# The first value block of a decode-attention kernel loaded by every eighth row instead of by column halves

## The chip, the cores and the metric

The kernel runs on one NeuronCore of a Trainium2 chip. The metric is device time in microseconds (us), from start to end of one execution; the median of several runs is given. The core has engines that run side by side: TensorE (PE, matrix products; PEld is its weight load), VectorE (DVE), ScalarE (ACT), GpSimd (POOL) and SyncE (SP), which here only issues loads. Loads and stores are carried out by 16 DMA engines that all issuing queues share.

## The reference

One query row per head attends to 8192 keys; there are 16 heads of 256 elements, all bfloat16.

```
B, H, Sq, Sk, D = 1, 16, 1, 8192, 256
scale = q.shape[-1] ** -0.5
scores = jnp.einsum("bhqd,bhkd->bhqk", q, k) * scale
p = _softmax(scores, axis=-1)
return jnp.einsum("bhqk,bhkd->bhqd", p, v)
```

Keys and values are 4 MB each per head, 134 MB together, and each byte is used once.

## The kernel before

**Layout.** The 8192 keys of a head are dealt to 128 partitions, 64 consecutive keys to each: partition p holds keys 64p to 64p + 63, which is one run of 64 x 256 elements or 32 KB in memory. J = 64 is the number of keys of a partition, D = 256 the elements of one. A "column" j of a block is the j-th key of every partition. There are two buffers for K and two for V (`kbuf`, `vbuf`); even heads use the first, odd heads the second.

**Work per head.** VectorE multiplies 48 of the 64 columns of K with the query and sums them (L191). TensorE does the other 16: it transposes them (L280), ScalarE copies the transposes out of the accumulators (L376), and TensorE multiplies them with the query (L294). VectorE takes the maximum (L207), TensorE transposes and broadcasts it (L228, L234) with a step of VectorE between (`xmax`, L173), ScalarE forms the exponentials and their sum. Then `pv` on TensorE (L259) adds up 64 products, one for each column of V, and ScalarE scales the row and stores it (`final`, L401). In one turn of TensorE's loop the order is: scores of an even head, `pv` of the even head two before, scores of the odd head, `pv` of the odd head two before. Within `pv` of an even head the maximum of the following odd head is transposed after 32 columns and broadcast after 48. VectorE's part of that broadcast, `xmax` of the odd head, comes after its column 40 of the next even head.

**The loads.** SP issues all loads of K and V from one list, `stream` (L57 to L71), in the order of the list, and the DMA engines carry them out in that order. An entry names the tensor, the head, the columns and the semaphore that counts its landing; each transfer adds 16. Heads 0 and 1 go into empty buffers. From head 2 on, the load of K waits until VectorE has finished with the buffer (`kd`), and the load of V until `pv` has (`pv`). The list begins: K0 in three pieces (columns 0 to 15, 16 to 31, 32 to 63), K1, the first half of V0's columns, K2, the second half of V0, the first half of V1, K3, the second half of V1; then K(h + 2) and V(h) in turn for h = 2, 3 and so on. V14 and V15, the last two, come in four and nine pieces of columns.

**The waits of `pv`.** The same code runs for all heads. It waits for `va0` or `va1` (the whole block, or its first piece), and then, before certain columns, for further semaphores of pieces (`v0c` before column 32 and so on; `V_SEMS`, `V_LATE`). Blocks that come whole need no such wait; GpSimd adds 16 to the piece semaphores once at the start (the list `late`), so that the waits pass for all heads but the last two. `v0c` and `v1c` are not in `late`, since V0's and V1's second halves add the 16 themselves.

Of the kernel before, what the change touches and what calls it, by code (L numbers as in the profile page):

```python
# [13 lines left out]
K_FIRST = (16, 32)  # L14
# [3 lines left out]
V_SEMS = (("va0", "v0b", "v0c", "v0d"), ("va1", "v1b", "v1c", "v1d", "v1e", "v1f", "v1g", "v1i", "v1j"))  # L18
# [22 lines left out]
def bass_standalone__mha_softmax__decode_kernel(nc: bass.Bass, q: bass.AP, k: bass.AP, v: bass.AP, out: bass.AP):  # L41
    B, H, Sq, D = q.shape
    Sk = k.shape[2]
    P = 128
    J = Sk // P
# [4 lines left out]
    JD = J - NPE  # L50
    QW = D + NH
    HALF = J // 2
    dt = k.dtype

    stream = [("k", 0, 0, K_FIRST[0], "k0"), ("k", 0, K_FIRST[0], K_FIRST[1], "k0a")]  # L57
    stream += [("k", 0, K_FIRST[1], J, "k0b"), ("k", 1, 0, J, "k1")]
    stream += [("v", 0, 0, HALF, "va0"), ("k", 2, 0, J, "k0"), ("v", 0, HALF, J, "v0c")]
    stream += [("v", 1, 0, HALF, "va1"), ("k", 3, 0, J, "k1"), ("v", 1, HALF, J, "v1c")]  # L60
    for h in range(2, H):
        if h + 2 < H:
# [4 lines left out]
        elif h == V_HALVED:  # L67
            stream += [("v", h, 0, HALF, "va1"), ("v", h, HALF, J, "v1h")]
        else:
            stream.append(("v", h, 0, J, f"va{h % 2}"))  # L70

    with contextlib.ExitStack() as ctx:

        def sb(name, shape, d):
            return ctx.enter_context(nc.sbuf_tensor(name, shape, d))
# [6 lines left out]
        def sem(name):  # L82
            if name not in sems:
                sems[name] = ctx.enter_context(nc.semaphore(name))
            return sems[name]

        kbuf = [sb(f"kbuf{i}", [P, J * D], dt) for i in range(2)]
        vbuf = [sb(f"vbuf{i}", [P, J * D], dt) for i in range(2)]
# [25 lines left out]
            sem(name)  # L114
        for name in ("l", "rc", "pv", "fin", "ldq", "k0", "k0a", "k0b", "k1", "va0", "va1", "v1h", "o0", "o1"):
            sem(name)
        late = [name for row in V_SEMS for name in row[1:] if name not in ("v0c", "v1c")] + ["v1h"]
        for row in V_SEMS:
            for name in row[1:]:
                sem(name)  # L120
# [1 line left out]
        def src(t, h):  # L122
            return t[0, h].rearrange("(p j) d -> p (j d)", p=P)

        if True:

            @(lambda f: f(nc.sync))
            def _(sp):
                for kind, h, a, b, name in stream:
                    buf = (kbuf if kind == "k" else vbuf)[h % 2]  # L130
                    if h >= 2 and a == 0:
                        if kind == "k":
                            sp.wait_ge(sem("kd"), h)
                        else:
                            sp.wait_ge(sem("pv"), h + 1)
                    sp.dma_start(  # L136
                        buf[:, a * D : b * D], src(k if kind == "k" else v, h)[:, a * D : b * D]
                    ).then_inc(sem(name), 16)
                sp.nop()
# [85 lines left out]
            def _(pe):  # L225
# [26 lines left out]
                def pv(h, waits, at):  # L252

                    pe.wait_ge(sem("fin"), h.of(1, 3))
                    pe.wait_ge(sem(f"va{h.par}"), h.of(8, 32 - 8 * h.par))
                    for j in range(J):
                        for name, value in waits.get(j, ()):
                            pe.wait_ge(sem(name), value)
                        ins = pe.matmul(  # L259
                            acc[h.par][0:1, 0:D],  # L260
                            lhsT=E[h.par][:, j : j + 1],
                            rhs=vbuf[h.par][:, j * D : (j + 1) * D],
                            start=(j == 0),
                            stop=(j == J - 1),
                        )
                        if j == J - 1:
                            ins.then_inc(sem("pv"), 1)
                        if j + 1 in at:
                            at[j + 1]()
# [76 lines left out]
                with pe.Fori(0, H // 2 + 1) as i:  # L346
                    ev, od = _Step(0, i), _Step(1, i)
                    fin_turn = pe.snap((i // 8) * 16 + 16)
                    half_turn = pe.snap(((i + 1) // 8) * 16 + 16)
                    old = od.back(2)  # L350
                    with pe.If(i < H // 2):
                        scores(ev)
                    with pe.If(i > 0):
                        pv(
                            ev.back(2),
                            {V_LATE[14][n]: [(V_SEMS[0][n], fin_turn)] for n in range(1, len(V_SEMS[0]))},
                            {32: lambda: transpose_m(old), 48: lambda: bcast(old), 64: lambda: total(old)},
                        )
                    with pe.If(i < H // 2):
                        scores(od, before=ev)  # L360
                    with pe.If(i > 0):
                        waits = {V_LATE[15][n]: [(V_SEMS[1][n], fin_turn)] for n in range(1, len(V_SEMS[1]))}
                        waits[HALF] = [("v1h", half_turn)]
                        pv(old, waits, {})
                    with pe.If(i < H // 2):
                        total(ev)
# [122 lines left out]
```

## Time and profile before

| | us |
|---|---|
| median of 3 runs | 320.06 (320.04 to 320.07) |
| the profiled execution | 320.12 |
| its span | 318.6 |
| VectorE busy | 275.2 (86%) |
| TensorE busy, weight loads | 219.2 (69%), 156.0 (49%) |
| ScalarE busy | 92.5 (29%) |
| bytes moved by the loads and stores | 134.29 MB, mean 422 GB/s |

The span runs from the first to the last instruction on the core; the execution's own time adds what lies around it. Busy times of different engines overlap. A row of a timeline gives the start, the time taken, the engine, the line of the kernel, the operation with the tile written and the tiles read, and the count; what stands in brackets is the idle time before it and what ended that. "SPq" is SP issuing loads: its time is that of issuing, not of the transfer. A row of the issues gives tensor, queue, count, KB of one and the median time from issue to landing in us. A row of the stretches gives its limits, its length, the busy time of each engine with the number of instructions, the granted TensorE clock, the busy share of the DMA engines and the rate in GB/s; a share may pass 1 a little, since an engine has more than one packet under way.

### The profile page before, as it was taken

How to read it: one execution, taken by the hardware profiler on the slowest of the kernel's cores; microseconds unless marked ns; L12 is line 12 of the kernel's file. 1: busy time of each engine (PE TensorE's matmuls, PEld its weight loads, DVE VectorE, ACT ScalarE, POOL GpSimd, SP SyncE). 2: the span in 40 equal slices, each digit the busy share in tenths (PEclk: the TensorE clock that was granted, in tenths of full speed). 3: DMA queues.
4: the chain of work that ended last, by engine and by line, in shares of the span. 5: the costliest groups of instructions: out<-in, count | busy, mean ns of one | idle time of the engine just before them, and what ended most of it. 6: DMA issues, size and time to landing. Idle time of an engine off the chain costs nothing.

```text
span 318.6 us, 6833 instructions
## 1 busy us (share of the span) xinstructions
PE 219.2 (69%) x2163; PEld 156.0 (49%) x2163; DVE 275.2 (86%) x1584; ACT 92.5 (29%) x172; POOL 1.6 (0%) x11
## 2 busy tenths in 40 slices
PE   4446185988775947949387482975739668497987
PEld 1335163656553634727256262663626446266664
DVE  3989999999999898897988979799798897979920
ACT  5436050333215050330505114051330603306010
POOL 1000000000000000000000000000000000000000
PEclk9999999659797875957879597695977859699999
DMA  7999999999999999999999999999999999999995
GB/s 303 447 418 465 393 455 407 448 416 448 412 448 428 428 444 411 453 412 453 420 436 440 416 448 407 453 416 449 424 432 444 411 449 416 444 405 428 419 416 201
DMA packets 6981, 134.29 MB, mean 422 GB/s; under 512 B 800, under 2 KB 1216, under 8 KB 1856
## 3 DMA queue, kind: packets, MB, share of 16 engines
q1 hardware_dynamic: 6912, 134.22, 98.6%
q8 instruction: 2, 0.03, 0.0%
q10 hardware_dynamic: 64, 0.02, 0.0%
q14 instruction: 3, 0.02, 0.0%
HBM read 134.23 MB, written 0.01 MB: 421 GB/s over the span
## 4 chain that ended last, share of the span: by engine, by line
DMA 64%; PE 19%; DVE 15%; SPq 1%; issue 1%; ACT 0%; DVEq 0%; ACTq 0%
DMA vbuf<-in_v_dram 58%; PE acc L259 18%; DVE kbuf L191 14%; DMA kbuf<-in_k_dram 7%; SPq L136 1%; DVE S L191 0%; DVE g L173 0%; PE sm L234 0%; ACT o_sb L401 0%; DVE recip L178 0%; DVEq L209 0%; DVEq L183 0%; PE qps L244 0%; DVE m L207 0%; ACTq L400 0%
## 5 line engine op out<-in xcount | busy, mean ns | idle before, releaser
L191 DVE CUSTOM_DVE_ANT_0 kbuf<-kbuf,q_now 128x256 bf16<-128x256 bf16 x768 | 268.4, 409 | 21.3 <-DMA kbuf<-in_k_dram 20.4
L259 PE MATMUL acc<-vbuf,E 128*1 128x256 bf16 x1024 | 147.1, 313 | 41.6 <-DMA vbuf<-in_v_dram 41.4
L259 PEld LDWEIGHTS acc<-vbuf,E 128*1 128x1 bf16 x1024 | 95.5, 95 | 86.2 <-DMA vbuf<-in_v_dram 44.4
L376 ACT ACTIVATE KT<-tp 128x1024 bf16<-128x1024 bf16 x64 | 62.3, 1021 | 46.4 <-PE tp L280 45.9
L191 DVE DVE_READ_ACCUMULATOR2_ANT S<- 128x1 f32 x768 | 55.2, 72 | 0.0
L280 PE MATMUL tp<-identb,kbuf 128*128 128x128 bf16 x512 | 42.2, 239 | 14.7 <-DMA kbuf<-in_k_dram 14.5
L280 PEld LDWEIGHTS tp<-identb,kbuf 128*128 128x128 bf16 x512 | 33.6, 107 | 18.1 <-DMA kbuf<-in_k_dram 12.1
L294 PE MATMUL spe<-q_now,KT 128*128 128x1 bf16 x512 | 22.9, 166 | 27.3 <-ACT KT L376 27.0
L294 PEld LDWEIGHTS spe<-q_now,KT 128*128 128x128 bf16 x512 | 18.1, 99 | 35.7 <-ACT KT L376 26.1
L401 ACT ACTIVATE o_sb<-acc,recip 1x256 bf16<-1x256 f32 x16 | 7.3, 458 | 87.0 <-PE acc L259 85.7
L384 ACT ACTIVATE negb<-sm 128x1 f32<-128x1 f32 x16 | 2.8, 174 | 83.8 <-PE sm L234 83.8
L173 DVE TENSOR_REDUCE g<-mx 1x1 f32<-1x128 f32 x16 | 4.4, 276 | 7.5 <-PE mx L228 7.5
L234 PE MATMUL sm<-g,ones_row 1*128 1x1 f32 x32 | 6.5, 268 | 5.0 <-DVE g L173 5.0
L228 PE MATMUL mx<-ident,m 128*1 128x128 f32 x32 | 6.5, 287 | 4.3 <-DVE m L207 4.3
L234 PEld LDWEIGHTS sm<-g,ones_row 1*128 1x128 f32 x32 | 5.1, 198 | 7.1 <-DVE g L173 5.6
L371 ACT ACTIVATE q_now<-q_all 128x258 bf16 x16 | 6.7, 418 | 0.1
L178 DVE RECIPROCAL recip<-qps 1x1 f32<-1x1 f32 x16 | 2.4, 152 | 3.9 <-PE qps L244 3.9
L388 ACT ACTIVATE E<-S,negb 128x64 bf16<-128x64 f32 x16 | 5.6, 348 | 0.5
L336 PE MATMUL acc<-q_sb,identb 16*128 16x256 bf16 x16 | 4.3, 404 | 0.8 <-ACT q_all L426 0.8
L228 PEld LDWEIGHTS mx<-ident,m 128*1 128x1 f32 x32 | 2.1, 82 | 5.1 <-DVE m L207 4.8
L426 ACT ACTIVATE q_all<-acc 128x512 bf16<-128x512 f32 x8 | 4.3, 592 | 0.6 <-PE acc L336 0.6
L380 ACT ACTIVATE S<-spe 128x16 f32<-128x16 f32 x16 | 2.9, 184 | 3.6 <-PE spe L294 3.6
(24 smaller groups left out, 18.5 us busy)
## 6 DMA issues: line engine op xcount, KB each, us to landing
kbuf<-in_k_dram SPq DMA_DIRECT2D x15, 4096.0 KB, 20.3
vbuf<-in_v_dram SPq DMA_DIRECT2D x11, 4096.0 KB, 28.7
vbuf<-in_v_dram SPq DMA_DIRECT2D x6, 2048.0 KB, 24.4
vbuf<-in_v_dram SPq DMA_DIRECT2D x5, 1024.0 KB, 14.8
kbuf<-in_k_dram SPq DMA_DIRECT2D x2, 1024.0 KB, 5.8
kbuf<-in_k_dram SPq DMA_DIRECT2D x1, 2048.0 KB, 11.3
vbuf<-in_v_dram SPq DMA_DIRECT2D x1, 768.0 KB, 10.2
vbuf<-in_v_dram SPq DMA_DIRECT2D x1, 640.0 KB, 11.3
```

The costliest lines, as they stand in the source:

```text
L173: dve.tensor_reduce(g[0:1, h.par : h.par + 1], mx[0:1, 0:P], AX.X, ALU.max).then_inc(sem("g"), 1)
L191: ins = dve.tensor_tensor_reduce(out=buf[:, j * D : (j + 1) * D], in0=buf[:, j * D : (j + 1) * D], in1=q_now[h.par][:, 0:D], scale=SCALE, ...
L228: pe.matmul(mx[0:1, 0:P], lhsT=m[:, h.par : h.par + 1], rhs=ident[:, :], start=True, stop=True).then_inc(sem("mT"), 1)
L234: pe.matmul(sm[:, 0:1], lhsT=ones_row[0:1, 0:P], rhs=g[0:1, h.par : h.par + 1], start=True, stop=True,).then_inc(sem("bc"), 1)
L259: ins = pe.matmul(acc[h.par][0:1, 0:D], lhsT=E[h.par][:, j : j + 1], rhs=vbuf[h.par][:, j * D : (j + 1) * D], start=(j == 0), stop=(j == J ...
L280: ins = pe.transpose(tp[gi % 2][:, b * D + hf * P : b * D + (hf + 1) * P], buf[:, j * D + hf * P : j * D + (hf + 1) * P], identb[:, :],)
L294: ins = pe.matmul(spe[:, c : c + 1], lhsT=KT[gi % 2][:, b * D + hf * P : b * D + (hf + 1) * P], rhs=q_now[h.par][:, D + hf : D + hf + 1], ...
L336: ins = pe.matmul(acc[pair % 2][:, (h % 2) * D : (h % 2 + 1) * D], lhsT=identb[0:H, h : h + 1].to_broadcast([H, P]), rhs=q_sb[:, :], start ...
L371: act.activation(out=q_now[h.par][:, :], in_=src_q, func=ACT.Copy).then_inc(sem("qb"), 1)
L376: act.activation(out=KT[gi % 2][:, :], in_=tp[gi % 2][:, :], func=ACT.Copy).then_inc(sem("kt"), 1)
L388: act.activation(out=E[h.par][:, :], in_=S[h.par][:, :], func=ACT.Exp, bias=negb[:, h.par : h.par + 1], scale=1.0, accum_out=lsum[:, h.par ...
L401: act.activation(out=o_sb[h.par][0:1, :], in_=acc[h.par][0:1, 0:D], func=ACT.Copy, scale=recip[0:1, h.par : h.par + 1],).then_inc(sem("fin ...
```

## The change

V0, the value block of head 0, is no longer loaded as two halves of columns into all 128 partitions (128 x 16 KB each). It is loaded by eight transfers. Transfer r takes the partitions r, r + 8, r + 16 and so on to r + 120, 16 of them, with their whole 32 KB. Transfer 0 stands at the very head of the list, ahead of K0; transfers 1 to 3 stand behind K1, where the first half was; transfers 4 to 7 behind K2, where the second half was. All eight count on `va0`, so that `pv` of head 0 waits for 144 (16 from GpSimd and eight times 16) before its first column, and the values of later even heads rise by the same amount. `v0c` joins the semaphores that GpSimd raises ahead. All else is as before; lines further down move by 6.

```
@@ -50,13 +50,15 @@
     HALF = J // 2
+    ROWS = P // 16
...
-    stream = [("k", 0, 0, K_FIRST[0], "k0"), ("k", 0, K_FIRST[0], K_FIRST[1], "k0a")]
+    stream = [("row", 0, 0, 1, "va0")]
+    stream += [("k", 0, 0, K_FIRST[0], "k0"), ("k", 0, K_FIRST[0], K_FIRST[1], "k0a")]
     stream += [("k", 0, K_FIRST[1], J, "k0b"), ("k", 1, 0, J, "k1")]
-    stream += [("v", 0, 0, HALF, "va0"), ("k", 2, 0, J, "k0"), ("v", 0, HALF, J, "v0c")]
+    stream += [("row", 0, 1, ROWS // 2, "va0"), ("k", 2, 0, J, "k0"), ("row", 0, ROWS // 2, ROWS, "va0")]
...
-        late = [name for row in V_SEMS for name in row[1:] if name not in ("v0c", "v1c")] + ["v1h"]
+        late = [name for row in V_SEMS for name in row[1:] if name != "v1c"] + ["v1h"]
...
                 for kind, h, a, b, name in stream:
+                    if kind == "row":
+                        for r in range(a, b):
+                            sp.dma_start(vbuf[0][r:P:ROWS, :], src(v, h)[r:P:ROWS, :]).then_inc(sem(name), 16)
+                        continue
...
-                    pe.wait_ge(sem(f"va{h.par}"), h.of(8, 32 - 8 * h.par))
+                    pe.wait_ge(sem(f"va{h.par}"), h.of(8, 144 - 120 * h.par))
```

## The prediction

> **What bounds the kernel now.** I read the page first: the busy times, the forty slices with their DMA rows, the queues and the shares of the chain.
>
> ```profile
> span 318.6 us, 6833 instructions
> PE 219.2 (69%) x2163; PEld 156.0 (49%) x2163; DVE 275.2 (86%) x1584; ACT 92.5 (29%) x172; POOL 1.6 (0%) x11
> ...
> DMA  7999999999999999999999999999999999999995
> ...
> q1 hardware_dynamic: 6912, 134.22, 98.6%
> ...
> DMA 64%; PE 19%; DVE 15%; SPq 1%; issue 1%; ACT 0%; DVEq 0%; ACTq 0%
> ```
>
> The 16 DMA engines are full in every slice but the first and the last: SP's queue moves 134.22 MB and its packets fill 98.6% of the span. VectorE has 14% to spare, TensorE more. To price bytes I took stretches of the busy times: the start, the long middle, the end (the last column is GB/s).
>
> ```profile
> 0.00:2.50 2.50, 0.00 (x0) 0.00 (x0) 0.00 (x0) 1.28 (x1) 1.56 (x11) 1.00 0.35 53
> 2.50:5.00 2.50, 1.29 (x7) 0.62 (x7) 0.00 (x0) 0.83 (x4) 0.00 (x0) 1.00 0.96 396
> ...
> 82.50:302.50 220.00, 155.78 (x1568) 111.84 (x1569) 198.71 (x1145) 59.91 (x114) 0.00 (x0) 0.80 1.00 431
> 302.50:314.50 12.00, 10.92 (x95) 7.32 (x92) 2.00 (x12) 1.08 (x4) 0.00 (x0) 1.00 1.00 404
> ```
>
> 134.22 MB at the 431 GB/s of the middle take 311.4 us. The load stream begins near 2 us and ends near 314.5, so under 2 us of it are idle. The chain's last pieces show what follows the loads:
>
> ```profile
> 312.33 1.25 PE acc L259 x10
> ...
> 313.62 3.28 PE acc L259 x26
> ...
> 316.97 0.47 ACT o_sb L401
> ```
>
> Head 15's value products run behind its last chunks. This tail hangs on the last loads, so whatever makes the load stream longer makes the span longer by the same time.
>
> **The change, part by part.** The reader needs where SP issues what, and when it lands: first SP's queue in order of time, then issues with their time to landing (K1, V0's first half, K2, K3, V1's second half, K4; each line from a short stretch around its issue).
>
> ```profile
> 0.74 2.03 SPq L136 DMA_DIRECT2D kbuf<-in_k_dram  x4
> 2.81 0.44 SPq L136 DMA_DIRECT2D vbuf<-in_v_dram  x1
> 22.26 0.33 SPq L136 DMA_DIRECT2D kbuf<-in_k_dram  x1
> 22.63 1.79 SPq L136 DMA_DIRECT2D vbuf<-in_v_dram  x2
> 40.27 0.33 SPq L136 DMA_DIRECT2D kbuf<-in_k_dram  x1
> 40.64 0.43 SPq L136 DMA_DIRECT2D vbuf<-in_v_dram  x1
> 57.96 0.33 SPq L136 DMA_DIRECT2D kbuf<-in_k_dram  x1
> 59.69 0.33 SPq L136 DMA_DIRECT2D vbuf<-in_v_dram  x1
> 75.69 0.33 SPq L136 DMA_DIRECT2D kbuf<-in_k_dram  x1
> ```
>
> ```profile
> kbuf<-in_k_dram SPq DMA_DIRECT2D x1, 4096.0 KB, 21.1
> vbuf<-in_v_dram SPq DMA_DIRECT2D x1, 2048.0 KB, 26.0
> ...
> kbuf<-in_k_dram SPq DMA_DIRECT2D x1, 4096.0 KB, 16.5
> ...
> kbuf<-in_k_dram SPq DMA_DIRECT2D x1, 4096.0 KB, 18.0
> vbuf<-in_v_dram SPq DMA_DIRECT2D x1, 2048.0 KB, 22.5
> ...
> kbuf<-in_k_dram SPq DMA_DIRECT2D x1, 4096.0 KB, 14.9
> ```
>
> So K1 lands near 23.2, K2 at 38.8, K3 at 58.3, V1's second half at 63.1, K4 at 72.9: always in the order of issue, without a gap.
>
> *The shape of the transfers.* Two transfers of 128 partitions x 16 KB go; eight of 16 partitions x 32 KB come, at partitions r, r+8, ..., r+120. Bytes stay 4,194,304, and at 431 GB/s those take 9.73 us. What the trace lacks is a large load into 16 partitions. Its one load into 16 is that of q, from ACT's queue:
>
> ```profile
> q_sb<-in_q_dram ACTq DMA_DIRECT2D x1, 8.0 KB, 2.9
> ```
>
> The lower end is the rate of the full transfers, 0 us extra. The upper end is eight times q's time, if rows went one after another at that price: 8 x 2.9 = 23.2 us, 13.5 more than 9.73. Between them stands a factor of two, 19.46 us, 9.73 more. [...] I take the factor of two: its 19.46 us lies nearer to q's 23.2 than 9.73 does. This is weak, since most of q's 2.9 us is the latency of a small load; hence the wide range below.
>
> [...]
>
> *More and smaller transfers.* 8 instead of 2. The stretch at the end, 302.5 to 314.5, moved by V15's chunks of 1024 KB and less, ran at 404 instead of 431 GB/s; at 404 V0 takes 10.38 us, 0.65 more. That is the upper end, and part of it is the stream running out; the lower end is 0. Rows of 512 KB in 32 KB packets are nearer to the middle's full rows: I take 0.1.
>
> *The first row ahead of K0.* From 2.5 to 5 us the engines move 396 GB/s, 35 below the middle: 35 x 2.5 / 431 = 0.2 us. [...] For both I take -0.3 together; the ends are 0 and -1.3 (second rival). K0 and K1 come later by row 0's time, 1.2 us alone, 2.4 doubled. VectorE's start moves with them, and so does the issue of K2 at 22.26, which waits for VectorE to finish head 0: near 24.7. Then K1 is still under way (23.2 + 2.4 = 25.6), and rows 1 to 3 stand behind it: no gap.
>
> *SP's queue.* Row 0's issue precedes K0's; V0 transfers took 0.44 (the first) and a share of 1.79 (the second). Eight issues at about 0.43 are 3.4 us instead of about 1.3, spread over 0.7, 4 and 25 us. Rows 1 to 3 are issued while K0 and K1, 8 MB or 19.5 us of loads, flow; rows 4 to 7 and V1's first half while rows 1 to 3 and K2 flow. K3 behind them waits for VectorE until past 40 anyway. Cost 0; without that cover, 2.1 us. POOL sends one signal more (v0c's, now ahead of time), before anything needs it: 0.
>
> *The wait on TensorE.* Head 0's products wait for the whole of V0 (one count of 144) instead of half and half. TensorE in order of time:
>
> ```profile
> 44.79 5.16 PE L259 MATMUL acc<-vbuf,E 128*1 128x256 bf16 x32
> ...
> 50.00 1.91 PE L259 MATMUL acc<-vbuf,E 128*1 128x256 bf16 x16
> 55.57 0.58 PE L234 MATMUL sm<-g,ones_row 1*128 1x1 f32 x2 [3.66 <-DVE g L173]
> 56.09 3.57 PE L259 MATMUL acc<-vbuf,E 128*1 128x256 bf16 x16
> 59.45 0.23 PE L244 MATMUL qps<-ones_col,lsum 128*1 128x1 f32 x2
> ```
>
> Products 33 to 48 end at 51.9, and then TensorE waits 3.66 us for VectorE's maximum of head 1. That is the cover for up to 3.66 us. With doubled rows: K2 lands near 38.8 + 2.4 + 7.3 - 4.9 = 43.6 (row 0 and rows 1 to 3 doubled, V0's first half gone), V0 is whole near 53.4, 48 products take some 7 to 8 us, then come 16 more: done near 64 to 65 instead of 59.5. Queued behind are head 3's transposes, which wait for K3 (58.3 + 9.7 = 68), and V2's issue, which waits for these products: 59.69 becomes about 65. The DMA queue then still holds K3 until 68, V1's half until 72.8, K4 until 82.6: no gap. VectorE takes 17.7 us a head (K3's issue at 40.27 to K4's at 57.96, each at a head's end), so head 2 ends near 61, K3 is awaited until 68, head 3 ends near 85 instead of 75.69, and K5 is issued then; V2 lasts until about 92. From there the old rhythm runs 9.5 us late.
>
> *Sum.* 9.73 + 0.1 - 0.3 = 9.5 us on the profiled execution's own 320.12 us (span 318.6); the median of the runs shown, 320.06, is 0.06 below it. 320.06 + 9.5 = **329.6 us**, 3.0% slower.
>
> **Rivals.**
> 1. *Rows run at full rate.* [...] For it: at 431 GB/s an engine moves 27 GB/s whatever the packet. Against: no load in the trace shows it for 16 partitions. 0.1 more for the transfers and up to 0.2 less at the start: 320.0, within 319.5 to 320.6. [...]
> 2. *Faster: the start is filled.* Place: 0 to 5 us. [...] In the first 2.5 us 53 GB/s move 0.13 MB; a stream at 431 from 1.3 us would have moved 0.52, 0.9 us more. With the ramp's 0.2 and some for landing, 1.3 us at most: 318.8. It decides from 0.64 us on, and only if rows run at full rate. Against: K0's issue starts at 0.74 already, and a first row has the same way to go.
> [...]
> 4. *Worse than double*, up to q's price: 320.06 + 13.5 = 333.6.
> 5. *The whole-V0 wait binds.* Products of head 0 would have to end over 17 us late (V2 issued after K4's 82.6 instead of near 65) before the DMA queue runs dry. Its price before that is 0.
>
> **How the numbers follow.** Doubled rows 0.74, with a range of their own from 328.5 to 330.4 (320.06 + 9.73 - 1.3 + 0, and 320.06 + 9.73 + 0.65 - 0). Full rate 0.11; faster start 0.06; partly doubled 0.06; worse than double 0.03; the wait under 0.01, counted with the worse. The range from 323 to 331.5 leaves out full rate, the faster start and the worse: 0.20. A measurement of this kernel tells 0.2%, 0.64 us. Faster 0.06 (second rival), same 0.11 (first), slower 0.83.
>
> **What would show it.** Right: two stretches near half the rate, about 25.6 to 33 and 43.6 to 53.4 us, at some 215 GB/s with the DMA share still near 1 (packets last twice as long); K2 landing near 43.6, K3 near 68; VectorE waiting 6 to 7 us for K3; then 431 GB/s, and the same tail 9.5 us later. The full rate would show as some 430 GB/s in both stretches and K3 near 58. A stretch of low DMA share behind K4 would show the wait of rival 5. [...]

## The result and the profile after

| | before | changed |
|---|---|---|
| median of 6 runs each, us | 320.15 (320.04 to 320.24) | 334.7 (334.25 to 335.95) |
| ratio, 95% interval | | 1.0464 (1.0452 to 1.0476) |
| the profiled execution, its span, us | 320.12, 318.6 | 334.25, 332.8 |

The change costs 14.5 us, 4.6%. The forecast was 9.5 us, and its range ended at 331.5. The page of the changed kernel, with the lines that answer to those shown of before:

```profile
span 332.8 us, 6840 instructions
PE 220.4 (66%) x2163; PEld 156.6 (47%) x2163; DVE 275.2 (83%) x1584; ACT 92.7 (28%) x172; POOL 1.6 (0%) x11
...
DMA  7998999999999999999999999999999999999995
GB/s 240 454 436 189 421 205 223 463 419 416 437 433 441 441 429 425 417 433 437 441 437 433 414 425 433 441 441 437 433 410 429 433 441 441 433 412 419 420 413 192
...
q1 hardware_dynamic: 6880, 134.22, 98.5%
...
DMA 62%; PE 19%; DVE 15%; issue 1%; SPq 1%; ACT 1%; DVEq 0%; ACTq 0%
```

Bytes and busy times of the engines are what they were. The DMA engines are as full as before (98.5% of a longer span), yet three slices move 189, 205 and 223 GB/s. An engine that is busy and moves half is an engine whose packets last twice as long. The stretches of the busy times (last columns: granted clock, DMA share, GB/s) place it. A packet counts there with its whole time and all its bytes in the stretch in which it starts (the 16 that start from 2.0 to 3.5 us count 0.52 MB and a share of 1.50 there); this is the main reason why the share of a short stretch can lie above or well below 1 (1.19 and 0.45 below) and why its GB/s scatter:

```profile
0.00:2.50 2.50, 0.17 (x1) 0.12 (x2) 0.00 (x0) 1.28 (x1) 1.56 (x11) 1.00 0.81 187
2.50:5.00 2.50, 2.12 (x11) 0.75 (x9) 0.00 (x0) 2.00 (x6) 0.00 (x0) 1.00 0.45 95
...
25.00:30.00 5.00, 3.02 (x28) 2.24 (x28) 2.73 (x15) 1.63 (x2) 0.00 (x0) 1.00 1.02 210
30.00:35.00 5.00, 3.31 (x44) 2.76 (x44) 5.00 (x31) 3.32 (x8) 0.00 (x0) 1.00 0.72 210
...
40.00:45.00 5.00, 0.00 (x0) 0.00 (x0) 4.52 (x27) 0.00 (x0) 0.00 (x0) 1.00 1.19 334
45.00:50.00 5.00, 1.52 (x15) 1.52 (x16) 1.54 (x10) 0.45 (x1) 0.00 (x0) 1.00 0.91 184
50.00:55.00 5.00, 3.44 (x52) 2.74 (x49) 5.00 (x29) 3.98 (x6) 0.00 (x0) 1.00 1.00 210
55.00:60.00 5.00, 1.87 (x9) 1.09 (x10) 5.00 (x31) 0.17 (x1) 0.00 (x0) 1.00 0.91 321
60.00:65.00 5.00, 5.00 (x29) 3.13 (x28) 2.86 (x19) 0.00 (x0) 0.00 (x0) 1.00 1.04 446
...
100.00:300.00 200.00, 138.25 (x1384) 98.66 (x1383) 178.95 (x1032) 54.11 (x103) 0.00 (x0) 0.78 1.00 431
```

Rows 1 to 3 run at 210 GB/s, rows 4 to 7 at 184 to 210, and from 60 us on the kernel is as before. In the records of the single packets a row packet of 32 KB lasts 2.54 us where rows alone are under way; away from the rows nearly all 32 KB packets last 1.22. Where rows and full transfers meet stand packets that belong to neither picture. Joined end to start, the records give the order on each engine: three engines still have a packet of K1 when most others are in row 1, and it lasts 1.9 to 2.5 us. Packets around the start of row 4 last up to 3.3 us, and a third of V1's first 16 KB packets last 1.2 us instead of 0.61.

SP's queue, the landings of K2, K3, V1's second half and K4, and K1's row in the chain show where the delay builds up:

```profile
24.92 0.33 SPq L142 DMA_DIRECT2D kbuf<-in_k_dram  x1
...
44.32 0.33 SPq L142 DMA_DIRECT2D kbuf<-in_k_dram  x1
44.70 0.43 SPq L142 DMA_DIRECT2D vbuf<-in_v_dram  x1
67.64 0.33 SPq L142 DMA_DIRECT2D kbuf<-in_k_dram  x1
68.81 0.33 SPq L142 DMA_DIRECT2D vbuf<-in_v_dram  x1
89.58 0.33 SPq L142 DMA_DIRECT2D kbuf<-in_k_dram  x1
```

```profile
kbuf<-in_k_dram SPq DMA_DIRECT2D x1, 4096.0 KB, 23.5
...
kbuf<-in_k_dram SPq DMA_DIRECT2D x1, 4096.0 KB, 28.1
vbuf<-in_v_dram SPq DMA_DIRECT2D x1, 2048.0 KB, 32.7
...
kbuf<-in_k_dram SPq DMA_DIRECT2D x1, 4096.0 KB, 19.4
```

```profile
3.02 24.24 DMA kbuf<-in_k_dram
```

| lands near, us | before | forecast | changed |
|---|---|---|---|
| K1 | 23.2 | 25.6 | 27.3 |
| K2 | 38.8 | 43.6 | 48.4 |
| K3 | 58.3 | 68 | 72.4 |
| V1, second half | 63.1 | 72.8 | 77.4 |
| K4 | 72.9 | 82.6 | 87.0 |

From K3 on the delay is 14.1 to 14.3 us and stays, and the span is 14.2 us longer. The tail behind the loads did not change: the same groups of 10 and 26 products and the same store, each some 14.2 us later.

```profile
326.55 1.25 PE acc L265 x10
...
327.82 3.29 PE acc L265 x26
...
331.18 0.47 ACT o_sb L407
```

### The profile page after: what moved, and what is told of

Same layout as the page of the kernel before. It is cut to its first block, busy times and chain, and to the rows that moved or that the text cites. A ratio compares the mean times of both kernels' runs of the same rounds, so it can differ in the third digit from the quotient of the medians.

```text
span 332.8 us, 6840 instructions
## 1 busy us (share of the span) xinstructions
PE 220.4 (66%) x2163; PEld 156.6 (47%) x2163; DVE 275.2 (83%) x1584; ACT 92.7 (28%) x172; POOL 1.6 (0%) x11
## 3 DMA queue, kind: packets, MB, share of 16 engines
q1 hardware_dynamic: 6880, 134.22, 98.5%
## 4 chain that ended last, share of the span: by engine, by line
DMA 62%; PE 19%; DVE 15%; issue 1%; SPq 1%; ACT 1%; DVEq 0%; ACTq 0%
DMA vbuf<-in_v_dram 46%; PE acc L265 18%; DMA kbuf<-in_k_dram 16%; DVE kbuf L197 14%; SPq L142 1%; ACT KT L382 1%; DVE S L197 1%; PE sm L240 1%; PE mx L234 0%; PE tp L286 0%; PE spe L300 0%; DVE g L179 0%; SPq L134 0%; ACT o_sb L407 0%; DVEq L189 0%
## 5 line engine op out<-in xcount | busy, mean ns | idle before, releaser
L286 PEld LDWEIGHTS tp<-identb,kbuf 128*128 128x128 bf16 x512 | 33.6, 107 | 32.8 <-DMA kbuf<-in_k_dram 23.2
L213 DVE TENSOR_REDUCE m<-S 128x1 f32<-128x64 f32 x16 | 3.5, 220 | 0.5
```

What stands on the lines that cost most here:

```text
L286: ins = pe.transpose(tp[gi % 2][:, b * D + hf * P : b * D + (hf + 1) * P], buf[:, j * D + hf * P : j * D + (hf + 1) * P], identb[:, :],)
```

## The experiments

Theory at the start: the doubled time of row packets comes from the destination (which partitions a transfer writes; "write paths" in the expectations), and something at the borders of a stretch of rows adds to it. Rivals: the source (reads 256 KB apart), and the number of transfers. Times are medians of four runs, each beside runs of the kernel before (320.15 to 320.19).

### Same places and number, other shape, source or destination

Eight transfers of columns into all partitions:

```
-  sp.dma_start(vbuf[0][r:P:ROWS, :], src(v, h)[r:P:ROWS, :])
+  c = slice(r * (J // ROWS) * D, (r + 1) * (J // ROWS) * D)
+  sp.dma_start(vbuf[0][:, c], src(v, h)[:, c])
```

> Eight transfers in the same places as the changed kernel, but each of 8 columns into all 128 partitions (4 KB packets) instead of 16 whole partitions. Write paths (the cost lies in which partitions a transfer reaches): the loss goes, 320.2 to 321.0 us (0.65 us at most for smaller transfers). Number (the cost lies in eight transfers instead of two, their issue and their completions): 334 to 335 us as in the changed kernel. Source stride: 320.2 to 321.0, since the rows of the source are read as before.

320.86 us, ratio 1.0019 (1.0005 to 1.0033). The place ahead of K0, the order, the eight issues, the eight completions and the wait of head 0's products for the whole of V0 cost 0.6 us together by the ratio, even with 4 KB packets. The number is out.

Neighbouring rows of the source, destination as changed:

```
-  sp.dma_start(vbuf[0][r:P:ROWS, :], src(v, h)[r:P:ROWS, :])
+  sp.dma_start(vbuf[0][r:P:ROWS, :], src(v, h)[16 * r : 16 * r + 16, :])
```

> Destination as in the changed kernel (partitions r, r + 8, ...), source 16 neighbouring rows of V0, 512 KB in one piece, instead of rows 256 KB apart; head 0's values therefore stand in other partitions than its weights. Write paths: 334 to 335.5 us, as changed. Source stride (reads 256 KB apart disturb one another): 320 to 322 us. Number: 334 to 335.5.

334.73 us, the same as the changed kernel. The source is out.

Source as changed, neighbouring partitions as destination:

```
-  sp.dma_start(vbuf[0][r:P:ROWS, :], src(v, h)[r:P:ROWS, :])
+  sp.dma_start(vbuf[0][16 * r : 16 * r + 16, :], src(v, h)[r:P:ROWS, :])
```

> Source as in the changed kernel (rows r, r + 8, ...), destination 16 neighbouring partitions 16 r to 16 r + 15; head 0's values therefore stand in other partitions than its weights. [...] Source stride or number: 334 to 335.5, as changed. [...]

347.69 us, 27.5 us over before: row packets last 3.9 to 4.3 us instead of 2.54. Two stretches each of the columns, of the near source and of the near destination, in this order:

```profile
25.00:30.00 5.00, 4.69 (x55) 4.13 (x53) 5.00 (x30) 3.12 (x4) 0.00 (x0) 1.00 1.13 472
...
40.00:45.00 5.00, 3.92 (x55) 3.31 (x53) 4.47 (x27) 3.99 (x4) 0.00 (x0) 1.00 1.08 446
```

```profile
25.00:30.00 5.00, 3.43 (x32) 2.77 (x31) 3.21 (x18) 1.94 (x2) 0.00 (x0) 1.00 1.01 206
...
50.00:55.00 5.00, 3.53 (x53) 2.84 (x50) 5.00 (x31) 3.98 (x6) 0.00 (x0) 1.00 0.94 200
```

```profile
55.00:60.00 5.00, 0.79 (x8) 0.79 (x9) 0.81 (x5) 0.00 (x0) 0.00 (x0) 1.00 0.89 118
60.00:65.00 5.00, 3.92 (x56) 3.31 (x54) 5.00 (x30) 3.99 (x4) 0.00 (x0) 1.00 0.88 118
```

At a DMA share of 0.9 to 1, the destination alone turns about 431 GB/s into 206 and, with 16 neighbours, into 118: half and about a quarter. The columns run at the full rate (472 and 446).

### Four transfers of every fourth partition, behind K2

Three kernels load all of V0 behind K2: as eight rows in a run, as four transfers of 32 partitions, and as one full transfer.

```
-  ROWS = P // 16
+  ROWS = P // 32          # only in the four; the count that pv waits for follows
-  stream = [("row", 0, 0, 1, "va0")]
...
+  stream += [("k", 2, 0, J, "k0"), ("row", 0, 0, ROWS, "va0")]   # the full one: vbuf[0][:, :]
```

> All eight row transfers in one run behind K2, none ahead of K0, none behind K1. Write paths with a price at each border between rows and full transfers (the 3.9 us that the changed kernel lost beyond the doubling, at three stretches): one stretch instead of three and no later start, 320.15 + 9.7 + 0.9 (packets of 2.54 instead of 2.43 us) + about 1 = 331 to 332.5. If the excess belongs to the row packets themselves, wherever they stand: 334 to 335.

> [...]

> V0 as one full transfer of 4 MB behind K2, so in the place of the run of eight and of the four of stride 4, without any rows. If that place itself costs time, because nothing but K1 stands in front of K2 and SP issues K2 only when VectorE has finished head 0 (22.6 us), the DMA engines run dry: 321.8 to 322.3 us, and the four transfers of stride 4 (322.1) lose nothing by their shape. If the place is free: 320.2, and stride 4 costs 1.9 us by its shape.

The run of eight took 332.46 us (331.97 to 334.64, the profiled one the slowest), the four 322.09, the full transfer 322.04. So the place costs 1.9 us by itself, and the shape of the four costs nothing: 32 partitions four apart are written at the full rate. A stretch in which the four are under way; their 32 KB packets last 1.22 us:

```profile
35.00:40.00 5.00, 3.46 (x43) 3.20 (x44) 5.00 (x29) 2.22 (x3) 0.00 (x0) 0.50 1.01 428
```

The stretches from 20 to 25 us, first before, then the four, show the place's price (TensorE's granted clock differs, 1.00 and 0.50; the run of eight, at 1.00, has the same 229 and 210 GB/s there):

```profile
20.00:22.50 2.50, 0.00 (x0) 0.00 (x0) 2.45 (x15) 0.00 (x0) 0.00 (x0) 1.00 0.78 334
22.50:25.00 2.50, 2.34 (x18) 1.71 (x18) 1.63 (x10) 0.68 (x1) 0.00 (x0) 1.00 1.00 419
```

```profile
20.00:22.50 2.50, 0.00 (x0) 0.00 (x0) 2.46 (x15) 0.00 (x0) 0.00 (x0) 0.50 0.54 229
22.50:25.00 2.50, 2.14 (x17) 1.64 (x18) 1.43 (x9) 0.48 (x1) 0.00 (x0) 0.50 0.75 210
```

With nothing of V0 between K1 and K2, SP has nothing queued when K1 ends and K2's wait is still open; (334 + 419 - 229 - 210) x 2.5 / 431 = 1.8 us are lost. Against the full transfer in its own place, the run of eight costs 332.46 - 322.04 = 10.4 us in the median: no excess over the doubled packets, 128 x (2.54 - 1.22) / 16 = 10.6. My reading of 1.7 us for its borders, which later expectations quote, was wrong: that was the place. The profiled execution, at 334.64 us, does pay more: 12.5 us over the full transfer's profiled 322.10. In it one engine pauses for 0.7 us in K2 and still has a packet of K2 when the other 15 begin their first row within 0.5 us of each other; packets of up to 3.5 us follow.

### None ahead of K0, and the rows in alternating order

```
-  stream = [("row", 0, 0, 1, "va0")]
...
-  stream += [("row", 0, 1, ROWS // 2, "va0"), ("k", 2, 0, J, "k0"), ("row", 0, ROWS // 2, ROWS, "va0")]
+  stream += [("row", 0, 0, ROWS // 2, "va0"), ("k", 2, 0, J, "k0"), ("row", 0, ROWS // 2, ROWS, "va0")]
```

> Rows 0 to 3 behind K1, rows 4 to 7 behind K2, none ahead of K0: two stretches of rows instead of three (changed) or one (the run of eight, 332.5). Price by stretch: between the two, 333 to 334 us. If only the row at the start was at fault for the excess (later start of 0.36 us and slower first packets): 332 to 332.5. No such price: 334 to 335.

334.7 us, as the changed kernel, which the expectation gives for no price by stretch. The runs below give another reason: both kernels have two stretches in mid-stream, and a stretch at the start costs no more than its own packets.

```
-  for r in range(a, b):                           # the run of eight behind K2
+  for r in (0, 4, 1, 5, 2, 6, 3, 7)[a:b]:
```

> The run of eight behind K2 with the rows in the order 0, 4, 1, 5, 2, 6, 3, 7 instead of 0 to 7. [...]

330.32 us, 2.1 us better than in order. Row packets last 2.24 us instead of 2.54: part of the doubling is gone. Why, the runs do not show.

### The rows as extra work

To measure the shape and the borders apart from the start of the kernel, the kernel before got 4 MB more to load, into a spare tile: one row behind each of V3 to V10; all eight rows behind V6; all eight ahead of K0; one full transfer behind V6.

```
+  if 3 <= h < 11:                                  # spread; the runs: if h == 6, rows 0 to 8
+      stream.append(("row", 0, h - 3, h - 2, "sp8"))
...
+  sp.dma_start(spare[r:P:8, :], src(v, h)[r:P:8, :]).then_inc(sem(name), 16)   # full: spare[:, :]
```

> The kernel before with 4 MB more to load: the eight row transfers of head 0's values once more, into a spare tile that nothing reads, one behind each of V3 to V10. Doubling alone: 320.2 + 8 x 2.54 = 340.5 us. With a price at each stretch's borders like the run of eight's (332.5 - 320.2 - 10.6 = 1.7 us): 340.5 + 8 x 1.7 = 354. If the load stream has slack in the middle: below 340.

> The same 4 MB more, all eight row transfers in one run behind V6. Doubling alone: 340.5 us; with one price at the borders, 342 to 342.5; below the spread one by seven such prices, or equal to it if borders cost nothing.

> The same 4 MB more as one full transfer of 128 partitions x 32 KB behind V6. All theories: 320.2 + 9.73 = 329.9 us, if the load stream is the bound in the middle as well; the run of eight minus this one is the price of the rows' shape alone.

> The eight extra rows into the spare tile as one run ahead of K0 instead of behind V6 (342.5 us): a stretch that has full transfers on one side only. 320.2 + 128 packets of 2.54 us over 16 engines (20.3) + the later start (0.36) = 340.8. If the price of about 2 us per stretch arises where full packets of the lagging engines meet the first rows: 340.8. If it arises where the last rows meet the full packets behind: 342.5 to 343. If by halves: 341.8.

| 4 MB more | us | over the full transfer |
|---|---|---|
| full, behind V6 | 329.9 | |
| eight rows ahead of K0 | 340.56 | 10.7 |
| eight rows behind V6 | 342.54 | 12.6 |
| a row behind each of V3 to V10 | 357.3 (ratio 1.116, 1.109 to 1.123) | 27.4 |

The full transfer came out at 320.2 + 9.73 to a tenth: the load stream is the bound in the middle too. The spread rows scattered most (355 to 361.5 us); their time in the table is the ratio times 320.15. Over the 10.6 us of doubled packets stand 0.1 us for the run at the start, 2.0 for the run in mid-stream, and 16.8 for eight single rows, 2.1 each. In these runs a stretch of rows in mid-stream costs about 2 us beside its packets, be it one row or eight; the one at the start costs none. The records show where the 2.0 us are. In the profiled run behind V6, 154 packets of 32 KB last over 1.9 us, though only 128 belong to rows: full packets beside the rows are slowed as well. Ahead of K0 it is 126.

### Idle engines in front of the rows

Last, the extra run and the extra full transfer again, but issued only when V6 has landed:

```
   if kind == "row":
+      sp.wait_ge(sem("va0"), 80)
```

> The eight extra rows behind V6 as in the run of eight (342.5 us), but SP issues them only when V6 has landed, so that all engines are idle and begin the rows together. Drift (the 2.0 us beyond the packets' own time come from engines that enter the rows at different times): the drained full transfer + 10.6 us. Border as such (rows beside full packets, whatever the engines' order): the drained full transfer + 12.6.

> The control of the drained run: the extra 4 MB as one full transfer, issued when V6 has landed. 329.9 us + what running dry costs, 1 to 3 us: 331 to 333.

343.04 and 332.49 us, 10.55 apart. Running dry costs 2.6 us (332.49 - 329.9), and with it the 2.0 us of the stretch are gone. The packet records say what differs. In the drained run and in the one ahead of K0 all 16 engines begin their first row within 0.9 us, and 126 packets last over 1.9 us in each. Behind V6 without the wait the first rows begin over up to 3.6 us, since some engines lag by a packet of V6 or more. Having been idle is not enough: in the profiled execution of the run behind K2 the engines had run dry some 10 us before the rows, and with its one late engine it still paid about 2 us more than the median. No trace shows the faster executions of that run, so that they were in step is a guess.

## Why the prediction was wrong

**The bound.** Right. What a transfer lost was found again at the end: 9.7 us for 4 MB more, 14.1 at K3 and 14.2 in the span.

**The shape of the transfers.** The factor of two was right, and the runs show what the trace before could not: it is the destination, not the source or the number. Why these partitions halve the rate is not shown. The term of 9.73 was a little small: the row packets' 2.54 us (210 GB/s, below half of 431) make it 10.6. The argument by q's 2.9 us for 8 KB had led to it by luck; that load is no measure of the rate of a large one: nearly all of its 16 packets of 512 bytes last 0.03 us, so most of the 2.9 is not their time.

**The step that failed** is the sum's last term, -0.3, which no run shows. With the row ahead of K0 and without it the time is the same (334.7 us both), and where engines came to the rows out of step the loss grew: 2.0 us for the extra run in mid-stream, 2.1 for a single row. Of the 5.0 us by which the forecast fell short, about 0.9 is the size of the doubling (10.6 instead of 9.73), and most of the rest is this price, for which the sum had no term.

In the changed kernel the price is not the same for each stretch. Summed over the packet records and shared among 16 engines, packets last longer than full ones by 1.0 us at the start, 4.7 around rows 1 to 3 and 7.8 around rows 4 to 7. That is 13.5 of the profiled execution's 14.1 us; 0.36 more is the later first packet. Doubled rows alone would be 1.3 each, so 4.0 and 5.3 for the two stretches in mid-stream: the borders cost 0.7 and 2.5 us there, and the row at the start nothing beyond its own packets. The kernel without the first row ahead has 0.8 and 2.5. So 10.6 + 2 x 2.0 = 14.6 comes near the measured 14.5, but its two equal parts are not what the trace has.

That the price goes when the engines start in step is shown (10.55 instead of 12.6), and so is that full packets beside rows last longer (154 slow packets where 128 are rows). The reason is not shown. The rows of the drained run also end closer together (within 1.4 us, against 3.7 behind V6 without the wait), so how much of the price belongs to each end of a stretch is open. Why it comes to 0.7 us at one stretch and to 2.5 at another, I did not settle.

**The start.** Wrong in sign, of little weight: the first packet starts 0.36 us later (2.10 instead of 1.74), and in the first 5 us 187 and 95 GB/s are counted where 53 and 396 were. Yet without the row ahead the time is the same, since that row then stands in mid-stream. The second rival, a filled start, is out: the first packet starts later, and rows run at 210 GB/s, not at the full rate it needs.

**More and smaller transfers.** 0.1 was taken, 0 to 0.65 allowed; eight transfers of columns measured 0.6.

**SP's queue and the wait on TensorE.** Right to cost nothing, though the eight issues took 5.4 us (0.57, 1.77 and 3.02) where 3.4 were expected. TensorE in order of time:

```profile
58.13 6.53 PE L265 MATMUL acc<-vbuf,E 128*1 128x256 bf16 x32 [3.62 <-DMA vbuf<-in_v_dram]
...
66.87 1.91 PE L265 MATMUL acc<-vbuf,E 128*1 128x256 bf16 x16
68.61 0.19 PE L250 MATMUL qps<-ones_col,lsum 128*1 128x1 f32 x2
```

Head 0's products begin at 58.1 (forecast 53.4) and end at 68.6 (64 to 65), and V2 is issued at 68.81, while loads are queued until K4's landing at 87: no gap, 446 GB/s from 60 to 65 us. The fifth rival had no part.

**The chances.** 0.83 for slower was right. The range took "worse than double" as 3 in 100 and ended below it, and even that rival's 333.6 was passed.

## What to carry to other kernels

A load that fills part of the partitions has to be judged by which partitions it writes, not by its bytes or by how many engines it runs on: here 16 partitions eight apart ran at half rate (210 GB/s), 16 neighbours at about a quarter (118), 32 four apart at the full rate (428), each at a DMA share of 0.88 to 1.02. In a kernel whose loads are the bound, such a transfer delays all that stands behind it in the queue (here K3 by 14.1 us and the store at the end by 14.2), and in mid-stream a stretch of them took 0.7 to 2.5 us more than its own packets. A DMA share near 1 with half the GB/s beside it (1.00 and 210 from 50 to 55 us) is the sign to look for.

## What was not expected of the hardware

A slow transfer costs its neighbours: single rows of 512 KB, 1.2 us at the full rate, cost 1.2 + 1.3 (the doubling) + 2.1 us (beside it) each when spread, so that eight of them apart took 27.4 us over a full transfer of the same bytes and eight in a run 12.6. And 32 partitions four apart lost nothing (322.09 against 322.04 us), though each such transfer, too, writes only a quarter of the partitions.
